# Fused linear attention and expert attention on one core: smaller q transfers, another q layout, g by a matmul, new orders

## The chip, the core and the metric

The kernel runs on one core of a Trainium2 chip. The core has a matrix engine (TensorE, PE in the profile), a vector engine (VectorE, DVE), a scalar engine (ScalarE, ACT), a general engine (GpSimd, POOL), an engine that only waits and issues transfers (SyncE, SP) and 16 DMA engines. Each engine works through its own list of instructions in order, and the engines meet at semaphores. The metric is the device time of one run in microseconds; lower is better.

## What is computed

Inputs are `q`, `k`, `v` of shape (8 batches, 8 heads, 576 tokens, 64), a norm weight `g_norm` of 64, and expert weights `w_gate` (512, 4), `wq`, `wk`, `wv` (4, 512, 64) and `wo` (4, 64, 512).

```
kv  = einsum('bhsd,bhse->bhde', k, v)
out = einsum('bhsd,bhde->bhse', q, kv)
x   = out / sqrt(mean(out*out, -1) + 1e-6) * g_norm        # heads joined: (8, 576, 512)
logits = x @ w_gate;  the two best of 4 experts per token, softmax over the two
for each expert e:
    a   = causal softmax((x @ wq[e]) @ (x @ wk[e]).T / 8)
    out += gate[e] * (a @ (x @ wv[e]) @ wo[e])
```

Each expert is an attention over all 576 tokens of a batch with one head of 64.

## The kernel before, in words

The work is cut into 1201 named tasks, each with a batch as its first number. Per batch: `lk`, `lv`, `lq` load; `kv` (two, `kv.b.n`) makes the 64x64 products on TensorE in fp32, `kvc` copies them out, `kgm` and `kgr` fold the gate weights in; `q` turns q on TensorE for batches 0 and 1 (`qc` copies the result), while for the other batches q comes in 32-float runs and `qc` turns it on VectorE; `out` multiplies by `kv`, five blocks of 128 tokens; `oc` copies, `sq` squares, `red` sums, `ln`, `rs` and three Newton steps `na`, `nb`, `nc` make the reciprocal root; `xm` scales, `x` turns on TensorE, `xc` copies. The gates are made from `gl`, `lg`, `m8` to `gate`. Then for two pairs of experts: `v`, `qp`, `kp` project, `sc` makes scores, `exp` and `msk` the masked exponentials, `pv` the weighted sums, `rc`, `iv`, `oc2` scale, `ot` turns, `y` multiplies by `wo`, `yc` copies, `st` stores.

Nothing is scheduled while the program is built. The string `ORDER` gives, two digits a task, the order in which the tasks are emitted, and so the order on every engine and on SP's queue of transfers. `ENGINE` gives for each task VectorE, ScalarE or GpSimd where it has a choice. `SLOTS` gives each buffer and each PSUM bank its place. A task waits for what it reads, and for the last user of the place that it writes. `ZEROS` names tasks before which TensorE gets a number of matmuls of zeros (128x512, bf16), written into the bank that the task writes next; they compute nothing that is used.

Loads are issued by SP (`lv` of batch 0 by ScalarE's queue). Batches 0 and 1 load k, v and q in two halves by head pair, in runs of 2304 bytes: nine tokens to a partition, so token 9p + j of a head lies in partition p at place j. All three `q_tr` of a batch read both halves. Batches 2 to 7 load k and v whole, and q in four quarters (32 partitions each, runs of 128 bytes). `gb` (L322) spreads the gate weights over the partitions with a matmul by a row of ones, and `wg` (L332) multiplies them by `g_wide`, which a transfer on GpSimd's queue fills in all 128 partitions (L197); `g8` (L318) scales `g_wide` and `g_rows` by 8. The weights `wq`, `wk`, `wv` are scaled by `g_rows` in `ws` (L345). Lines L267 and L270 are the helpers through which every matmul and every transpose of the end goes, L276 the one for copies, so in the profile the tiles tell them apart: `kvq` holds k, v, q and the turned q, `kvx` the products, `ident_f` is the fp32 identity that turns q.

Of the kernel before, what the change touches and what calls it, by code (L numbers as in the profile page):

```python
# [10 lines left out]
FP32 = mybir.dt.float32  # L11
# [12 lines left out]
    ('gb',): 19, ('q', 0, 2): 7, ('out', 0, 3): 9, ('q', 1, 2): 20, ('v', 0, 0): 1,  # L24
    ('sc', 0, 0, 0): 2, ('out', 1, 4): 6,
# [15 lines left out]
    "7J8pArAsANAd9HAt8t989I8uCQ9J99AO8vEJ8mAeASCRCE7MCIAh9ACFCMAfCJAgCUCGAiCNEKCKAjCVCH7PCOATELCS9KCLAU9L9MCPCWEO8w"
    "AoCT7SBMAp8y9N9PEM8x9O8zBNAw8+CXBK8-9QCYENAx9091CZAy9RBLCa92AkAzCb9S93AuAlCc9TGjBRCiB4AvGh9aBS9UCl9bCjB5EP9X9c"
    "BT9dCk9YCfCm9V9e9Z9gCrCnB79W9hB1B8BU9fGiB2CgB69iCsGgChD2B3CtBVCdD4D3D0D5D8D1BWCeBXA+D9B9BYBOCuA-BZEUCvCxEYCoCw"
    "BPGZCyEVB0EZEcBQCzEWC+GaC-EaEXEdEgEbGbEkEeEhCpElBAEiEfCqBbEmBCBBBDBfGcDCBEBgGeBhDcDDEjEnDaDdEoEpBFBaEqBGDbDAEr"
    "BcBHBdD6EsBeDBF2BIGfD7DnDhDoBJDHE-DiGdF3BiF4DIEtDkDEBjF0DlBtDjEuDJBnF1BuDpBqDmDFBoFMBvEyFKBrBpFNBkFLF8BsBwF5Bl"
    "EzBxBmDKE+F9DNDGByDeDLEvF6FIDODfFBGwF7DMFJGsGxFADPGkFCGtDgFDG+FEGlGuFFGoG-GvEwGmDrGpExDqGnDRGqFsDvDsGyGrDwDtGz"
    "H0FGDuFtFODxDQFHH1FPFqDSDVH2DTH3DWDUFSFrDXH4H5DYH6FTHCFQDZHFDyFRHDDzFxHEH9FuFyFUE7HID+FvE1D-E4FzE8E2HAFwE0E5H7"
    "HYE9HBHJHZE3FVHGHLE6HWHHEAHXHKFWFdFXEBFeHaH8FYECFfHcHOHMHRHbHPHdFZHQF+HNHSG1FaHTF-HUI8HVG2G0FbI6I9G3FcG5I7HgG9"
    "GAGBHiHhFgHjG4FhFiG6FjG7HeFkFlIDG8HfFmIEIGFnIAFoIBGCIFFpIJGDIKICIHHqHkILHnHrIIGHGNGIHoHsINGOGJGKHlHpIRGEGPGLIS"
    "IMGFITHmGQGMIOHtGRIPHwGGIQHuIWHvGSHyIXIUHzHxH+IVI2H-I0I3I1IbIYIcIeIZIdI4IfI5IaIkIhIgIlImIiIj"  # L50
)
ENGINE = (
    "VVVVVVVVVVVVVVVGVGVGVGVAVAVVVVVVVVVAVVVAVVAVVVGVVAAVVAAVVVGVAAVGVAAVGVAAVVVAAVVVAAVVVVVGVAGVAGVVGVVVVVVVAVVVVV"
    "VAVVVAVVVAVAVVVAGVAGVAGVAGVVVGVVGVVVVAVAVAGVAGVAGVAGVVVGVVGVVVVVVVAVVAVVVVVAVVVVVVVVVAGVGVVAVVVAVAAVVVAVVAGVVA"
    "AVVVAVAAVGVVVGVAGVAGVAGVVGVVVVAVVVVVVAVAVAVAVAVAVAVAGVAGVAGVAGVVVGVVVVVAVAVAVAGVAGVAGVAGVVVVVVVVVVVVVVAVVVVVVV"
    "VAVVVVVVVVVAGVVVVVVVVAGVVAAVVVAVVVGVVAAVAAVGVVVVVVGVVGVAVVAGVVVGAVGVVVVAVAVAVAVVVAVAVAGVAGVAGVAGVVVGVVGVVVVAVV"
    "VAGVAGVAGVAGVVVGVVGVVAVVVVAVVVVVAVVAVVVVVVVVVAGVGVVVVVVVGVVVGVVAAVVAGVVVGVAAVVVGVVVVGVAVVVGVAGVVVGAVGVVGVVVAVA"
    "VVVAVVVVVAGVAGVAGVAGVVVGVVGVVAVAVAVAGVAGVAGVAGVVVGVVVVVAVAVVAVVVVVVVVAVVVVVVVVVAGVGVVVVVVAGVVVAVVAAVVAAVVAGVAA"
    "VVVGVGVVVVAGVVGVVGVAVGAVGVVVVVVAVAVAVAVAVVVAGVAGVAGVAGVVVGVVVVVVVVVAVAGVAGVAGVAGVVVVVVGVVVVAVVVVVVVVVVVVVVVVVV"
    "VVVAGVGVVVVVVAAVVVAVVVAVVAGVVAAVAAVGVGVGVAGVVGVVVVAGVVVGAVVVVVVAVVVVVAVVVAVAVAGVAGVAGVAGVVVGVVGVVAVVVVVAGVAGVA"  # L60
    "GVAGVVVGVVGVVAVVVVVVVAVVAVVVVVVVVVVVVVVVGVVVVVVVAVVAAVVAGVVAGVVAAVAAVGVGVVVAGVVGVAGVVGVVVGAVGVVGVAVVVAVAVAVAVA"
    "VAGVAGVAGVAGVVVVVVVVVVVAVAVAGVAGVAGVAGVVVVVVVVVVVAVVVVVVVVVVVAVVVVVVVVVAVVGVVVVVVVGVVVAVVAAVVVAVVAAVAAVVVGVGVA"
    "VVVVVAGVAVVVVGAVGVVGVVVVVAVVVAVVVVVAGVAGVAGVAGVVVVVVGVVVVVVVVVVAGVAGVAGVAGVVVVVVGVVVVAVVVVAVVAVVVVVAV"
)
SLOTS = (
    "0120102341233450561677230120138021394A543B0102C30450106102101212011327603207301102102435202334015829BAC4163775"
    "40011132016752106123322013132081C4457671411037513200106200506131321300223145631440335102983BC415617110A7260127"
    "02231312520631020114312102161200432332649520376652B723010231021310320083321C0112011670072311047671B14AC5910305"
    "42136720132601132203103218012214025031545003452431071945BA2C302032301203012016170001166287060312726051742B1367"
    "1011297601230112231001106103223021067A2C61006111330010232248550174"  # L70
# [3 lines left out]
def loads(b):  # L74
    return range(EP) if b < 2 else range(1)


def names(nb):
# [3 lines left out]
    for b in range(nb):  # L82
        out += [(m, b, p) for p in loads(b) for m in ("lk", "lv")]
        out += [("lq", b, i) for i in (loads(b) if b in QPE else r4)]
        if b == 0:
            out += [("g8",), ("gb",), ("wg", 0), ("wg", 1)]
            out += [(m, nm, p) for nm in "qkv" for p in r2 for m in ("lw", "ws")]
            out += [(m, "o", p) for p in r2 for m in ("lwo", "wo")]
# [30 lines left out]
def kernel(  # L119
# [60 lines left out]
    def buf(key, shape, dtype, name):  # L180
# [7 lines left out]
    g_wide = const.tile([P, Dh], FP32, name="g_wide")  # L188
    ob = const.tile([P, NB, NCH, 2 * GW], FP32, name="o_sb")
# [4 lines left out]
    one_row = const.tile([1, Dh], FP32, name="one_row")  # L194
    nc.vector.memset(one_row[:], 1.0)
    nc.gpsimd.dma_start(wg_rows, moe_w_gate.rearrange("d e -> (d e)").unsqueeze(0))
    nc.gpsimd.dma_start(g_wide[:], g_norm.unsqueeze(0).to_broadcast([P, Dh]))  # L197
    nc.gpsimd.dma_start(
        g_rows[:], g_norm.rearrange("(p c) -> p c", c=NCH).unsqueeze(0).to_broadcast([P * NCH // Dh, Dh // NCH, NCH])
    )  # L200
# [107 lines left out]
    def lq(b, i):  # L308
        if b in QPE:
            load_nine(nc.sync, long("q", b), q, b, i)  # L310
            return
# [527 lines left out]
```

## Time and profile before

| what | value |
|---|---|
| median of 3 runs | 248.05 us (245.39 to 248.36) |
| the profiled execution's own time | 245.43 us |
| its span, first to last instruction | 243.6 us |
| mean granted TensorE clock | 0.934 |
| TensorE busy | 209.9 us, 86% |
| weight loads (overlap matmuls) | 170.8 us |
| VectorE, ScalarE, GpSimd busy | 163.1, 136.0, 112.5 us |
| matmuls of zeros | 64, 20.5 us |
| packets, bytes by DMA | 73225, 40.49 MB; 57024 packets under 512 B |
| read from and written to HBM | 30.45 MB, 9.44 MB |

Times in the profile are from one execution; its span starts at the first instruction. A row of a group gives the line in the kernel, the engine, what is written and read, how often, the busy time, the mean of one in ns, and the idle time ahead of it with what ended most of it. A busy share is an average over stages, so stages are read one by one. PE and PEld, matmuls and the loads of their stationary operand, are one list of instructions.

### The profile page before, as it was taken

To read this page: it belongs to the slowest core of one execution; us is meant where nothing else is said; L and a number is where in the kernel's file an instruction comes from. 1 tells how busy PE (TensorE), PEld (TensorE's weight loads), DVE (VectorE), ACT (ScalarE), POOL (GpSimd) and SP (SyncE) were. 2 spreads that over 40 slices of the span, in tenths; PEclk is the share of its full clock that TensorE was granted. 3 is DMA by queue.
4 is the path that set the end of the run, shared out by engine and by line. 5 is a ranking of instruction groups with operands and counts; after the bars stand their busy time and mean duration, and the time that the engine had idled before them with its cause. 6 is when DMAs were issued, how large, how long until landed. Compare 5 with 4: busy or idle time off the path is not lost.

```text
span 243.6 us, 9455 instructions
## 1 busy us (share of the span) xinstructions
PE 209.9 (86%) x4088; PEld 170.8 (70%) x4088; DVE 163.1 (67%) x408; ACT 136.0 (56%) x248; POOL 112.5 (46%) x203
## 2 busy tenths in 40 slices
PE   7948589799749779879998999699979999999992
PEld 2244438786616678879977968598869879889650
DVE  1066785315838934457999799379986889876582
ACT  2040615469615607733788378455875688793761
POOL 6007461018327237267456648243845673643330
PEclk9997979999968959689999999889999999999999
DMA  6999999999999969956981999600500050040055
GB/s 228 203 379 180 312 231 250 224 263 183 336 174 210 238 120 259 262 68 203 142 186 41 341 159 253 199 4 0 194 6 5 1 196 4 3 183 13 1 196 194
DMA packets 73225, 40.49 MB, mean 166 GB/s; under 512 B 57024, under 2 KB 59600, under 8 KB 73184
## 3 DMA queue, kind: packets, MB, share of 16 engines
q1 hardware_dynamic: 72544, 38.67, 63.9%
q10 hardware_dynamic: 544, 1.18, 1.3%
q0 software_dynamic: 96, 0.04, 1.2%
q8 instruction: 32, 0.52, 1.0%
q14 instruction: 9, 0.07, 0.1%
HBM read 30.45 MB, written 9.44 MB: 164 GB/s over the span
## 4 chain that ended last, share of the span: by engine, by line
PE 76%; issue 10%; DMA 5%; DVE 4%; ACT 3%; SPq 0%; ACTq 0%
PE p L267 74%; DMA kvq<-in_q_dram 5%; ACT PT L624 2%; PE p L270 2%; DVE osc L672 1%; DVE tmp L276 1%; DVE kvq L276 1%; DVE xT L276 1%; DVE OT L276 0%; DVE ms L446 0%; ACT qTp L276 0%; ACT o_sb L276 0%; ACT sq L440 0%; SPq L295 0%; DVE inv L661 0%
## 5 line engine op out<-in xcount | busy, mean ns | idle before, releaser
L624 ACT ACTIVATE PT<-p 128x1024 bf16<-128x1024 f32 (+1 forms) x64 | 50.3, 845 | 4.4 <-PE p L267 3.5
L630 POOL TENSOR_SCALAR_AFFINE_SELECT PT<-PT 128x256 bf16<-128x256 bf16 (+1 forms) x80 | 30.0, 395 | 36.5 <-ACT PT L624 36.3
L498 POOL TENSOR_TENSOR tmp<-o_sb,rstd 128x512 fp32r<-128x512 f32 x29 | 33.0, 1193 | 15.2 <-DVE rstd L477 9.7
L267 PE MATMUL p<-kvq,kvq 64*64 64x64 f32 x1152 | 23.3, 234 | 9.1 <-issue 9.0
L267 PE MATMUL p<-wv_r,xT 128*128 128x256 f32 x160 | 26.3, 300 | 2.4 <-issue 1.7
L267 PEld LDWEIGHTS p<-kvq,kvq 64*64 64x64 f32 x1152 | 21.2, 147 | 10.2 <-issue 9.8
L446 DVE TENSOR_REDUCE ms<-sq 128x8 f32<-128x520 f32 (+1 forms) x40 | 26.3, 678 | 1.9 <-POOL sq L442 1.4
L267 PE MATMUL p<-kvx,kvq 64*64 64x68 f32 x1152 | 24.3, 228 | 3.1 <-issue 3.1
L267 PEld LDWEIGHTS p<-kvx,kvq 64*64 64x64 f32 x1152 | 22.2, 139 | 5.3 <-issue 3.8
L267 PE MATMUL p<-ident_r,tmp 128*128 128x128 f32 (+1 forms) x160 | 24.6, 287 | 0.7 <-ACT PT L624 0.7
L267 PE MATMUL p<-zeros 128*128 128x512 bf16 x64 | 20.5, 480 | 5.4 <-issue 3.6
L442 POOL TENSOR_TENSOR sq<-o_sb 128x512 f32<-128x512 f32 (+1 forms) x15 | 15.5, 1038 | 20.5 <-ACT o_sb L276 10.2
L267 PEld LDWEIGHTS p<-ident_r,tmp 128*128 128x128 f32 x160 | 21.4, 198 | 4.3 <-issue 2.7
L267 PEld LDWEIGHTS p<-wv_r,xT 128*128 128x128 f32 x160 | 21.8, 196 | 3.5 <-issue 2.0
L276 ACT COPY o_sb<-p 128x544 f32<-128x544 f32 (+1 forms) x23 | 13.5, 609 | 18.0 <-PE p L267 17.6
L267 PE MATMUL p<-qTp,kT 64*128 64x64 f32 (+4 forms) x192 | 22.0, 344 | 0.7 <-ACT PT L624 0.7
L267 PE MATMUL p<-wo_b,OT 128*128 128x512 bf16 (+1 forms) x96 | 21.1, 375 | 1.5 <-DVE OT L276 0.9
L267 PE MATMUL p<-xT,wk_r 128*128 128x288 f32 x128 | 20.9, 312 | 0.0
L267 PE MATMUL p<-xT,wq_r 128*128 128x288 f32 x128 | 19.7, 299 | 0.0
L276 DVE COPY o_sb<-p 128x544 f32<-128x544 f32 (+1 forms) x17 | 12.0, 715 | 10.6 <-PE p L267 10.3
L267 PEld LDWEIGHTS <-zeros 128*128 128x128 bf16 x64 | 7.1, 119 | 16.9 <-issue 11.6
L267 PEld LDWEIGHTS p<-xT,wk_r 128*128 128x128 f32 x128 | 18.8, 201 | 0.3
(87 smaller groups left out, 354.9 us busy)
## 6 DMA issues: line engine op xcount, KB each, us to landing
out_dram<-tmp SPq DMA_DIRECT2D x32, 256.0 KB, 2.5
kvq<-in_q_dram SPq DMA_DIRECT2D x24, 288.0 KB, 8.0
kvq<-in_k_dram SPq DMA_DIRECT2D x6, 1152.0 KB, 8.1
kvq<-in_v_dram SPq DMA_DIRECT2D x6, 1152.0 KB, 7.3
kvq<-in_q_dram SPq DMA_DIRECT2D x4, 576.0 KB, 9.8
kvq<-in_k_dram SPq DMA_DIRECT2D x4, 576.0 KB, 11.1
kvq<-in_v_dram ACTq DMA_DIRECT2D x2, 576.0 KB, 9.2
kvq<-in_v_dram SPq DMA_DIRECT2D x2, 576.0 KB, 9.4
```

The source lines that it names most:

```text
L267: done.append(nc.tensor.matmul(*args, **kwargs))
L270: done.append(nc.tensor.transpose(*args))
L276: rd_(nc.scalar.copy(dst, src) if engine[task] == "A" else nc.vector.tensor_copy(out=dst, in_=src))
L442: nc.gpsimd.tensor_tensor(out=dst, in0=src, in1=src, op=AluOpType.mult)
L446: nc.vector.tensor_reduce(mss[b % 2][:nt, i, :], sqs[(NB * b + i) % 3][:nt], axis=AX_X, op=AluOpType.add)
L498: ew(("xm", b, i)).tensor_tensor(out=short("x", b, i, dtype=FP32R)[:].rearrange("p (c m k r) -> p m k r c", c=NCH, m=NCH, k=2), in0=ob[:, ...
L624: rd_(nc.scalar.activation(PT[:, :, d0 : d0 + o], big("sc", b, pr, j)[:, :, 0:o], ACTF.Exp, scale=scale))
L630: nc.gpsimd.affine_select(out=d, in_=d, compare_op=AluOpType.is_ge, fill=0.0, base=0, pattern=[[0, 2], [1, w]], channel_multiplier=-1,)
L672: rd_(nc.vector.tensor_tensor(out=osc[:, qc : qc + n, :, :].rearrange("p n e f -> p (n e) f"), in0=po[:, :, 0:Hd], in1=iv.rearrange("p n e ...
```

## The change

Five things change.

- `g_norm` comes into one partition (`g_row`). A new task `gg` spreads it with a matmul by ones into PSUM, and `g8` scales it from there into `g_wide`; a new task `g9` scales `g_rows`.
- q of batches 2 to 7 is loaded in eight transfers of 144 KB (two heads of a group each) where there were four of 288 KB; the runs stay 128 bytes.
- q of batches 0 and 1 is loaded in three parts of 192 tokens, each with two transfers (one for every half of the partitions) in runs of 768 bytes: three tokens to a partition. Token 192j + 3p + e lies in partition p. `q_tr` for part i reads that part alone, and writes PSUM with a step of three floats (`e::3`), so that the tokens stand in order there and `q_copy` reads and writes runs in order.
- `ORDER`, `ENGINE` and `SLOTS` are new throughout. TensorE's list now begins `gb` (14 zeros), `gg`, `kv.0.1`, `q.0.1`, `q.0.0` (6 zeros), `kv.0.0` (2), `q.0.2`, `out.0.2` (5), three more `out.0`, `q.1.2`, `out.0.4`, `x.0.0` (12), `q.1.0` (2), `x.0.2`, `v.0.0`, `kv.1.1`, the other `x.0`, `v.0`, `kp.0`, `qp.0`, two `sc`, `kv.1.0`, `q.1.1`. Before it began `gb` (19), the three `q.0` (7), both `kv.0`, `out.0` (9), the three `q.1` (20), two `x.0`, `kv.1.0`. SP's list begins `lk.0.1`, `lq.0.1`, `lq.0.0`, `lk.0.0`, `lq.0.2`, `lw.v.1`, `lw.k.1`, `lw.q.0`, `lq.1.2`, `lw.v.0`, `lw.q.1`, `lq.2.5`, `lk.1.1`, `lw.k.0`, `lq.1.0`, `lv.1.1`, `lk.1.0`, three eighths of `lq.2`, `lq.1.1`, `lq.3.7`, `lv.1.0`; nine transfers and weights later comes `lk.2.0`. On VectorE `qc.1.2` stands between `red.0.0` and `red.0.1`.
- 48 matmuls of zeros in nine places replace 64 in seven; `ot` may have them too.

```diff
 ZEROS = {
-    ('gb',): 19, ('q', 0, 2): 7, ('out', 0, 3): 9, ('q', 1, 2): 20, ('v', 0, 0): 1,
-    ('sc', 0, 0, 0): 2, ('out', 1, 4): 6,
+    ('gb',): 14, ('q', 0, 0): 6, ('kv', 0, 0): 2, ('out', 0, 2): 5, ('x', 0, 0): 12,
+    ('q', 1, 0): 2, ('sc', 0, 1, 2): 2, ('ot', 0, 1): 3, ('y', 0, 3): 2,
 }
...
-        out += [("lq", b, i) for i in (loads(b) if b in QPE else r4)]
+        out += [("lq", b, i) for i in (range(3) if b in QPE else range(8))]
         if b == 0:
-            out += [("g8",), ("gb",), ("wg", 0), ("wg", 1)]
+            out += [("gg",), ("g8",), ("g9",), ("gb",), ("wg", 0), ("wg", 1)]
...
+    g_row = const.tile([1, Dh], FP32, name="g_row")
...
-    one_row = const.tile([1, Dh], FP32, name="one_row")
+    one_row = const.tile([1, P], FP32, name="one_row")
     nc.vector.memset(one_row[:], 1.0)
+    nc.gpsimd.dma_start(g_row[:], g_norm.unsqueeze(0))
     nc.gpsimd.dma_start(wg_rows, moe_w_gate.rearrange("d e -> (d e)").unsqueeze(0))
-    nc.gpsimd.dma_start(g_wide[:], g_norm.unsqueeze(0).to_broadcast([P, Dh]))
...
     def lq(b, i):
         if b in QPE:
-            load_nine(nc.sync, long("q", b), q, b, i)
+            dst = long("q", b)[:].rearrange("p (m j x) -> p m j x", m=NCH, j=3)
+            src = q[b].rearrange("(m a) (j p e) d -> a j p m (e d)", a=2, j=3, p=NP)
+            for a in range(2):
+                nc.sync.dma_start(dst[a * Dh : (a + 1) * Dh, :, i, :], src[a, i])
             return
-        h0, a = NCH * (i // 2), i % 2
+        r, c0, n = i % 4, i // 4 * 2, 2 * (S // 32)
+        h0, a = NCH * (r // 2) + c0, r % 2
         nc.sync.dma_start(
-            long("q", b)[i * 32 : (i + 1) * 32].rearrange("p (x d) -> p x d", d=32),
-            q[b, h0 : h0 + NCH, :, a * 32 : (a + 1) * 32].rearrange("h (g t) d -> t (h g) d", t=32),
-        )
+            long("q", b)[r * 32 : (r + 1) * 32, c0 * S : (c0 + 2) * S].rearrange("p (x d) -> p x d", d=32),
+            q[b, h0 : h0 + 2, :, a * 32 : (a + 1) * 32].rearrange("h (g t) d -> t (h g) d", t=32),
+        )
+
+    def gg():
+        mm(small("gg")[:, 0:Dh], lhsT=one_row[0:1, :], rhs=g_row[0:1, :], start=True, stop=True)

     def g8():
-        for t in (g_rows, g_wide):
-            nc.vector.tensor_scalar_mul(out=t[:], in0=t[:], scalar1=float(Dh**0.5))
+        rd_(nc.vector.tensor_scalar_mul(out=g_wide[:], in0=small("gg")[:, 0:Dh], scalar1=float(Dh**0.5)))
+
+    def g9():
+        nc.vector.tensor_scalar_mul(out=g_rows[:], in0=g_rows[:], scalar1=float(Dh**0.5))
...
     def q_turned(b, i):
-        return big("qt", b, i)[:, :, 0 : 6 * NP].rearrange("p a (n j t) -> p a n j t", n=EP, j=3)
+        return big("qt", b, i)[:, :, 0 : 6 * NP].rearrange("p a (n t) -> p a n t", n=EP)

     def q_tr(b, i):
         t, p_t = nine(tiles["L", "q", b]), q_turned(b, i)
         for n in range(EP):
-            for j in range(3):
+            for e in range(3):
                 for a, o, rows, cols in quarters():
                     mm(
-                        p_t[cols, a, n, j, :], lhsT=t[rows, n + EP * o, 3 * i + j, :], rhs=ident_f[rows, rows],
+                        p_t[cols, a, n, e::3], lhsT=t[rows, n + EP * o, 3 * i + e, :], rhs=ident_f[rows, rows],
                         start=True, stop=True, skip_group_check=True,
                     )
...
-        dst = t[:].rearrange("p (n a t j) -> p a n j t", n=EP, a=2, j=NJ)[:, :, :, 3 * i : 3 * i + 3, :]
+        dst = t[:].rearrange("p (n a j t) -> p a n j t", n=EP, a=2, j=3)[:, :, :, i, :]
...
-        if n[0] in ("x", "v", "y"):
+        if n[0] in ("x", "v", "y", "ot"):
             t = small(*n)
```

## The prediction

> **What bounds the kernel now.** I read the page's busy shares and slices first, then a table of stages, the waits, the chain and the transfers.
>
> ```profile
> PE 209.9 (86%) x4088; PEld 170.8 (70%) x4088; DVE 163.1 (67%) x408; ACT 136.0 (56%) x248; POOL 112.5 (46%) x203
> ...
> PEclk9997979999968959689999999889999999999999
> DMA  6999999999999969956981999600500050040055
> ```
>
> TensorE leads. DMA is full for about 110 us, and the clock is low in that same stretch. The table has each stage's length, busy time by engine, granted clock, DMA share and GB/s:
>
> ```profile
> 0.00:13.68 13.68, 10.52 (x34) 3.61 (x35) 1.96 (x16) 1.28 (x1) 3.90 (x17) 1.00 0.86 237
> 13.68:39.09 25.41, 19.15 (x605) 12.90 (x605) 17.14 (x34) 8.97 (x18) 11.46 (x13) 0.87 1.00 259
> 75.00:110.00 35.00, 29.07 (x626) 27.02 (x627) 21.03 (x50) 18.46 (x36) 16.79 (x24) 0.80 0.90 196
> 160.00:227.30 67.30, 65.60 (x1090) 57.70 (x1083) 55.92 (x144) 46.13 (x84) 34.57 (x67) 1.00 0.16 55
> ```
>
> From 160 us TensorE has work at full clock all the time, so whatever it loses earlier moves the end. Its waits:
>
> ```profile
> PE p L267 <- issue: 17.5, 8, 3.6
> PE p L270 <- issue: 4.1, 1, 4.1
> PE p L267 <- ACT PT L624: 2.3, 5, 0.7
> PE p L267 <- DMA kvq<-in_q_dram: 1.9, 1, 1.9
> ```
>
> "issue" is a wait for no semaphore, and it is nearly all of the idle time. These stops come in the middle of groups (after one of five transposes of `ot`, for example). The trace gives them a rule: counted in weight loads, matmuls and waits, all the long ones stand at records 449, 961, 1473, 2497, 3009, 3777, 4801, 5569 and 6593, which is 193 plus a multiple of 256. They sum to 23.5 us from start to start. Each ends 1.3 to 1.7 us after a packet of the instruction queue:
>
> ```profile
> q8 instruction: 32, 0.52, 1.0%
> ```
>
> That is 16 KB a packet, 32 packets for 8228 records: 256 records each. A packet starts mostly 2 to 4 us after the boundary before it has been crossed while DMA is full (mostly 0 to 2 us later on). A block made of 64x64 matmuls alone runs in 2.1 to 2.9 us and so outruns it. What such a stop does is seen in the timeline:
>
> ```profile
> 31.58 5.32 PE L267 MATMUL p<-zeros 128*128 128x512 bf16 x18 [3.58 <-issue]
> 36.84 2.33 PE L267 MATMUL p<-ident_f,kvq 64*64 64x64 f32 x144
> 39.09 1.11 PE L267 MATMUL p<-ident_r,tmp 128*128 128x64 f32 x8
> ```
>
> The zeros before `q.1.2` run after the stop they were meant to fill. Batch 1's q had landed at 27.64 and the first `xm` was done at 33.0, yet batch 0's `x` starts at 39.1.
>
> **What the skill says.** "Runtime: NRT & Kernel Launch", Instruction fetch mechanics: refills of 16 KiB, 256 instructions, through a DMA queue. The trace agrees (193 + 256k); it does not agree that this is "mostly hidden". "TensorE: Matmul & The Clock Gate", Part 1: an idle window of about 3.4 us halves the clock. The trace has half clock for 3.4 or 6.8 us after the stops at 28, 66 and 84 us. "PSUM — Partial Sum Buffer", Specifications: lines of 8 bytes, and a non-contiguous pattern "slows matmuls significantly"; no row of before shows one.
>
> **Part by part.** *g.* The broadcast of `g_wide` goes. Its 16 packets took 1.51 us on average, and between 7 and 8 us only 4 load packets started where 138 to 174 did in each of the 4 us before. Worth 1.5 us for every later load. `gg` adds four records to TensorE and puts `g8` behind `gb`; it is ready at about 9.6 us, before `g9`'s data (12.59), so it costs nothing.
>
> *Loads.* Packets took 108 ns (2304 B), 57 ns (1024 B), 18 ns (128 B): a half of k or v is 256/16 x 108 = 1.7 us, a w 0.9, an eighth of q 1.3 (before: a quarter 2.6, so the sum is unchanged). For 768 B I estimate 46 ns between these rows (43 to 57): 4.4 us for a batch against 3.5. Batch 0, whole at 17.42 before with one w (0.9) ahead, is whole at 17.4 - 0.9 - 1.5 + 0.9 = 16. From there in SP's order `lv.1.1` lands at about 29, `lv.1.0` at 39, `lk.2.0` at 54. SP issues 60 q transfers for 28, 0.5 us each, hidden while DMA is behind; what then counts is that each load waits for the landing of the one eight places ahead (so the built program).
>
> *Start.* The first work needs only half of k and v, which take the places that landed at 6.25 and 6.73. 14 zeros at 0.43 us, `gb` 1.9, `gg`: `kv.0.1` runs at 9.6 (before: q at 13.68). Now the blocks decide. Boundary 193 lies at the end of `kv.0.1`, 10.7 us. With before's delays of crossing to crossing where a refill binds (4.8 to 6.5 us), 449 (in `kv.0.0`) is passed at 15.5, 705 (in `out.0.2`) at 20.8, 961 (in `q.1.2`) at 26.2. `out.0` is done by 27 against 27.4. So the earlier data is largely lost to refills.
>
> *`x` of batch 0.* VectorE has `qc.1.2` between its reductions, so `red.0.1` and all behind it (the Newton steps, `xm`) wait for `q.1.2`, 26.7 us. Then `qc` 1.0, two `red` 0.68 each, three small steps: `nc.0.0` at 29.5; `xm.0.0` 1.2: 30.7. TensorE has 12 zeros there, 2.6 us warm to 4.3 half cold after 27.0, so `x.0.0` starts at 31 (before 39.1). VectorE then needs two `red`, eight small steps, `xm.0.2`, two `ws` (0.74), `xm.0.1` (1.2), `vc`, `qc.1.0`, `xc.0.1`, `xm.0.4`: until about 40. `x.0.4` 40.5, its copy 41.1, four projections of 1.15 and one v: 46.4, two `sc`: 47. Before had this, and `q.1.1` besides (0.8), at 52.5. **Gain 4.7 us.** Of `kv.1` each has one half behind it.
>
> *Strided PSUM writes.* Six `q_tr` at 0.78 us. At most double by the two-float line: 4.7 us; batch 0's three lie in waits for data, so 0 to 2.3 on the path. I take 0.5. In return the copies write in order: 1.55 us for 768 elements now, about 0.9 to 1.0 by the 544-element row (0.61 on ACT, 0.72 on VectorE); counted above.
>
> *Zeros.* After this point before has 8 more (2.1 us), after 7 shorter waits of which some are filled: 0.6 gained. Those before `q.1.2` went into the 4.7. Zeros cannot fill a fetch stop, so "all longer gaps" is not what they reach.
>
> *Later stops.* Dense blocks (over 220 of 256 records of `kv`, `out`, `q`): before had stops of 4.36, 3.31, 1.78 and then 0, 0.97, 2.60, 1.92, 0, in all 14.9. After has blocks ending at 1729, 2497, 3009, 4033 in the full stretch (2.6, 1, 3.3, 2.5, from block time against 5.5) and about 2 at 1985 and 2241, and six later at before's mean of 1.1: 18.0. **Cost 3.1.** What it may give back is the clock: `y.0` took 4.5 us at half clock (0.7 of it a wait) against 2.3 for `y.1`, and 75 to 110 us ran at 0.80 (7 us lost). Smaller stops around 62 to 70 us leave `y.0` and `x.1` warm: I take 4.2 of these (0 to 9).
>
> Sum: 4.7 - 0.5 + 0.6 - 3.1 + 4.2 = 5.9. The profiled run's own time is 245.43 (span 243.6, 1.8 around it), so 239.5; the median of the three runs is 1.0107 times the profiled one, so **242.0**.
>
> **Rivals.** *More returns* (0.22): the clock stays up and DMA, rid of `g_wide`, refills sooner: another 5 to 8 us, 235. The stops stand for it, the number of dense blocks against. *Fetch takes it all* (0.13): the twelve dense blocks stop 4 us each while DMA is full; 247. The change then does not do what its zeros and orders are for. *The transfer queue runs dry* (0.17), the slower side: SP is in order, and blocked for a buffer (it stood 9.5, 8.8 and 11.6 us at 27, 46 and 63) it has eight eighths ahead, 10 us of work, where it had eight quarters, 21. TensorE reaches `kv.2.1` at about 62 with `lk.2.0` at 54, slack 8. If the DMA share of the first 60 us falls below 0.87, TensorE waits; at 0.71 it waits 9.4 and runs 3.4 us at half clock: 242 + 9.4 + 1.7 = 253. Full shares up to 108 us speak against. The forecast itself has 0.48, of which 0.31 below 243.1.
>
> **Numbers.** 2% (about what this kernel's measurement can tell from no change) is 243.1 and 253.0. Faster 0.31 + 0.22 = 0.53, same 0.17 + 0.13 = 0.30, slower 0.17. Range 233 (more returns at its best) to 252, leaving out most of the dry queue.
>
> **What would show it.** First `kv` matmuls at 9 to 10 us; no 2048-byte packets on the software queue; all long stops at 193 + 256k; `x.0` from 31, projections done by 47; DMA share near 1.0 to 100 us; `q_tr` still near 0.78 us. It fails if stops fall elsewhere, if `x.0` waits for VectorE well past 31, or if `kv` waits for k or v.

## The result, and the profile after

| | before | after |
|---|---|---|
| median of the runs, us | 246.77 (245.39 to 248.36, 4 runs) | 258.28 (256.24 to 258.89, 4 runs) |
| ratio, 95% interval | | 1.045 (1.035 to 1.055) |
| span of the profiled execution, us | 243.6 | 257.2 |
| mean granted TensorE clock | 0.934 | 0.933 |
| stops of TensorE that no semaphore explains, summed | 19.9 us, 8 stops | 33.3 us, 13 stops |

The change makes the kernel 4.5% slower; 242.0 was forecast, with a range up to 252. Ratios and intervals leave out slow runs, those over 1.5% above the quickest of the same kernel, unless they are said to be "by resampling", which takes all runs. The last row counts every gap over 0.25 us between the end of one matmul or weight load and the start of the next where the trace shows no semaphore.

The page of the changed kernel: busy times, the slices of clock and transfers, two queues, and the chain that ended last by engine.

```profile
PE 207.5 (81%) x4060; PEld 173.8 (68%) x4074; DVE 158.0 (61%) x399; ACT 138.9 (54%) x257; POOL 110.0 (43%) x203
...
PEclk9889777998999999989999599986999999999999
DMA  6999999999827999941949927993130041040046
...
q8 instruction: 32, 0.52, 1.0%
q0 software_dynamic: 96, 0.01, 0.3%
...
PE 63%; issue 16%; DVE 7%; DMA 6%; ACT 4%; POOL 2%; SPq 1%; DVEq 0%; POOLq 0%; ACTq 0%
```

TensorE works 2.4 us less than before and is still the longest engine; its share fell from 86% to 81% because it stands still more. The broadcast is gone from the software queue (0.3% for 1.2%), and there are as many instruction packets as before. Full stretches of transfers now last to about 175 us, where before the last load lands at 153.5, and they break off in places, longest from 109 to 122 us. TensorE's waits (us in total, times, longest):

```profile
PE p L270 <- issue: 34.1, 18, 5.8
PE p L270 <- DMA o_sb<-in_moe_w_gate_dram: 2.4, 1, 2.4
```

Where the time goes is read from four stages, cut where TensorE ends the projections of batches 0, 1 and 4. Columns: the stretch, its length, busy time of PE, PEld, DVE, ACT, POOL, granted clock, DMA share, GB/s. The kernel before:

```profile
0.00:51.80 51.80, 40.29 (x784) 26.79 (x784) 25.04 (x68) 16.20 (x29) 16.62 (x31) 0.93 1.00 260
51.80:95.10 43.30, 34.68 (x834) 28.10 (x833) 26.45 (x61) 23.22 (x44) 21.14 (x31) 0.84 0.97 213
95.10:167.80 72.70, 66.69 (x1380) 59.44 (x1379) 54.73 (x134) 44.92 (x84) 38.59 (x68) 0.93 0.74 162
167.80:243.60 75.80, 68.20 (x1099) 56.46 (x1096) 56.88 (x147) 51.61 (x91) 36.12 (x74) 0.99 0.23 80
```

The changed kernel:

```profile
0.00:55.00 55.00, 38.17 (x719) 28.06 (x723) 22.53 (x66) 13.42 (x31) 14.91 (x31) 0.88 1.06 217
55.00:93.80 38.80, 31.96 (x876) 27.44 (x879) 27.61 (x56) 23.90 (x45) 18.25 (x27) 0.96 0.82 202
93.80:182.40 88.60, 69.88 (x1386) 61.88 (x1386) 53.83 (x135) 49.37 (x90) 38.90 (x70) 0.90 0.74 165
182.40:257.20 74.80, 67.50 (x1086) 56.42 (x1089) 53.98 (x143) 52.19 (x93) 37.94 (x75) 1.00 0.23 81
```

So +3.2, -4.5, +15.9 and -1.0 us. In the third stage TensorE stands idle 18.7 us for 6.0 before, and 16.7 us of that are five such stops, for 4.7 in three before; the other 3.2 us are busy time, at a clock of 0.90 for 0.93. The worst stop is in the `kv` and `out` matmuls of batches 5 and 4. The timeline of TensorE there (start, length, operation, count, and the idle time before it):

```profile
129.93 2.21 PE L270 MATMUL p<-kvq,kvq 64*64 64x64 f32 x134
133.78 0.39 PE L270 MATMUL p<-kvq,kvq 64*64 64x64 f32 x10 [1.65 <-issue]
133.95 1.98 PE L270 MATMUL p<-kvx,kvq 64*64 64x68 f32 x118
141.72 1.41 PE L270 MATMUL p<-kvx,kvq 64*64 64x68 f32 x26 [5.79 <-issue]
```

Between the two stops lie 256 records, ten matmuls of `kv` and 118 of `out` with a weight load each. They run in 2.2 us, and then nothing is there to run for 5.8 us. The refill packet had started 5.0 us after the boundary at 133.8. (A boundary is the start of a block of 256 records; a refill is the packet of the instruction queue that brings the block after it; the rings, further down, are the lists of transfers that wait for the DMA engines.)

### The profile page after: what moved, and what is told of

It is laid out like the page before. It is cut to its first block, busy times and chain, and to the rows that moved or that the text cites. A ratio compares the mean times of both kernels' runs of the same rounds, so it can differ in the third digit from the quotient of the medians.

```text
span 257.2 us, 9446 instructions
## 1 busy us (share of the span) xinstructions
PE 207.5 (81%) x4060; PEld 173.8 (68%) x4074; DVE 158.0 (61%) x399; ACT 138.9 (54%) x257; POOL 110.0 (43%) x203
## 4 chain that ended last, share of the span: by engine, by line
PE 63%; issue 16%; DVE 7%; DMA 6%; ACT 4%; POOL 2%; SPq 1%; DVEq 0%; POOLq 0%; ACTq 0%
PE p L270 61%; DMA kvq<-in_k_dram 5%; ACT PT L636 2%; POOL tmp L510 2%; PE p L273 1%; DVE osc L684 1%; SPq L316 1%; DMA out_dram<-tmp 1%; DVE ms L458 1%; ACT tmp L279 1%; DVE rstd L489 1%; ACT xT L279 1%; DVE inv L673 1%; DVE tmp L510 1%; POOL tmp L396 0%
## 5 line engine op out<-in xcount | busy, mean ns | idle before, releaser
L270 PE MATMUL p<-kvx,kvq 64*64 64x68 f32 x1152 | 27.4, 243 | 13.5 <-issue 12.9
L270 PEld LDWEIGHTS p<-kvx,kvq 64*64 64x64 f32 x1152 | 24.9, 152 | 15.4 <-issue 13.5
L279 ACT COPY o_sb<-p 128x544 f32<-128x544 f32 (+1 forms) x28 | 16.6, 611 | 27.6 <-PE p L270 27.2
L270 PEld LDWEIGHTS p<-kvq,kvq 64*64 64x64 f32 x1152 | 20.0, 139 | 16.8 <-issue 16.1
L454 POOL TENSOR_TENSOR sq<-o_sb 128x512 f32<-128x512 f32 (+1 forms) x19 | 19.7, 1038 | 15.3 <-ACT o_sb L279 9.1
L270 PEld LDWEIGHTS p<-ident_r,tmp 128*128 128x128 f32 x160 | 20.8, 190 | 4.8 <-POOL tmp L510 3.0
L270 PE MATMUL p<-xT,wk_r 128*128 128x288 f32 x128 | 22.5, 323 | 1.0 <-DVE ms L458 0.7
L396 POOL TENSOR_TENSOR tmp<-kvx,wg_t 128x512 f32<-128x512 f32 x8 | 11.1, 1398 | 22.8 <-DVE kvx L279 17.9
L270 PEld LDWEIGHTS p<-xT,wk_r 128*128 128x128 f32 x128 | 19.6, 208 | 1.8 <-DVE ms L458 0.8
L673 DVE RECIPROCAL inv<-p 128x6 f32<-128x6 f32 (+1 forms) x32 | 5.9, 185 | 22.6 <-PE p L270 22.1
L270 PE MATMUL p<-vext,PT 128*128 128x65 bf16 x480 | 19.3, 201 | 0.2
L270 PEld LDWEIGHTS p<-qTp,kT 64*128 64x128 f32 x192 | 14.5, 185 | 7.1 <-DVE kvx L403 1.4
```

Source lines behind the costliest of these rows:

```text
L270: done.append(nc.tensor.matmul(*args, **kwargs))
L279: rd_(nc.scalar.copy(dst, src) if engine[task] == "A" else nc.vector.tensor_copy(out=dst, in_=src))
L396: ew(("kgm", b, m)).tensor_tensor(out=short("g", b, m)[:].rearrange("p (e f) -> p e f", e=E), in0=kvx[b % 2][:, m, E : E + 2 * Dh].unsquee ...
L454: nc.gpsimd.tensor_tensor(out=dst, in0=src, in1=src, op=AluOpType.mult)
L673: rd_(nc.vector.reciprocal(iv.rearrange("p n e -> p (n e)").unsqueeze(2), po[:, :, Hd : Hd + 1]))
```

## Experiments

The kernel before ran beside each group of experiments on the same chip, and the medians are given beside each other. In some groups its runs lay wide apart (238.0 to 251.7 us over 35 runs), so the intervals there are worked out by drawing anew from all runs of both kernels and taking the ratio of medians; this is said as "by resampling". Each experiment has one profiled execution, and single stops differ between executions, so one stop alone proves little.

### The order or the parts

`parts_only`: the order, slots and zeros of before, all three parts put in.

```diff
-            load_nine(nc.sync, long("q", b), q, b, i)
+            for j in {(0, 1): (2, 0), (0, 0): (1,), (1, 0): (2, 0), (1, 1): (1,)}[b, i]:
+                for a in range(2):
+                    nc.sync.dma_start(dst[a * Dh : (a + 1) * Dh, :, j, :], src[a, j])
...
+        for c0 in (0, 2):        # each quarter of q as two eighths, one after the other
...
+    gg, g8, g9 as in the change, gg after gb
```

> The order and the zero matmuls of the kernel before, with all three parts of the change: g by a matmul (w_gate fetched second), q of batches 2 to 7 in eighths, q of batches 0 and 1 in thirds of 768-byte runs with strided PSUM writes. Theory 'order' (the new order of the work lengthens the instruction-fetch stops): 241 to 248 us, no slower than before, fetch stops near the 21.6 us of before. Rival 'parts' (the smaller transfers, the 768-byte runs, the strided writes or the g matmul cost the time): 254 to 260 us, as the changed kernel.

`order_only`: the kernel before with `ORDER`, `ENGINE`, `SLOTS` and `ZEROS` of the change.

```diff
-ORDER, ENGINE, SLOTS, ZEROS of before
+those of the change, without gg, g9 and the second eighth of each quarter;
+lq.0.1, lq.0.0, lq.1.2, lq.1.0 load the halves, lq.0.2 and lq.1.1 nothing
```

> The changed kernel's order, engines, slots and zero matmuls, with none of the three parts: g broadcast by DMA, q of batches 2 to 7 in quarters (each issued where the first of its two eighths stood), q of batches 0 and 1 in two halves of 2304-byte runs, PSUM written in order. Theory 'order': 254 to 262 us, with fetch stops of about 33 us in all. Rival 'parts': 245 to 249 us, with stops near 22 us.

Beside 244.92 us of before, `parts_only` took 249.22 (ratio 1.022, 1.012 to 1.033; 1.018 by the medians) and `order_only` 252.18 (1.032, 1.024 to 1.041). Neither theory had it: by the medians they cost 4.3 and 7.3 us, and the sum is near the 11.5 of the change. The cost of the parts is the less certain of the two, as the runs further down show. In `order_only` TensorE has only 16.7 us of fetch stops, and in return waits 8.0 us for q. Its loss lies in the third stage all the same: 82.3 us for 72.7.

### Is it the instruction fetch, and where its boundaries lie

`shift128`:

```diff
-        for _ in range(count):
-            mm(t[:, :], lhsT=zeros[:, 0:P], rhs=zeros[:, 0:512], ...)
+        w = 512 if n != ("gb",) else 92        # and ZEROS: ('gb',): 14 -> 78
+        for _ in range(count):
+            mm(t[:, 0:w], lhsT=zeros[:, 0:P], rhs=zeros[:, 0:w], ...)
```

> The changed kernel with its 14 zero matmuls of 512 columns ahead of the first work replaced by 78 of 92 columns: the same length of time, 128 more instruction records, so that every 256-record boundary falls half a block earlier in the work. Theory 'fetch': all stops over 1.5 us without a semaphore again stand at records 193 + 256k, so they move to other tasks (the 5.8 us stop at the end of the batch-4 out group and the 4.9 us stop in out of batch 6 are gone from there), and the time changes by several us, 250 to 264. Rival 'program waits' (the stops belong to those tasks or to their buffers): they stay at the same tasks, with the same 5.8 and 4.9 us, and the time stays within 1 us of 258.

258.83 us (1.059, 1.051 to 1.066). All 14 stops stand at records 193 + 256k, now in other tasks. TensorE's timeline at the place of the 5.8 us stop:

```profile
136.44 1.77 PE L269 MATMUL p<-kvx,kvq 64*64 64x68 f32 x90 [1.02 <-issue]
138.14 1.30 PE L269 MATMUL p<-vext,PT 128*128 128x65 bf16 x37
142.78 0.43 PE L269 MATMUL p<-vext,PT 128*128 128x65 bf16 x5 [3.35 <-issue]
```

The 5.8 us stop is gone from its place in `out`, where 1.0 us stands some matmuls earlier, and 3.4 us sit in `pv`. The time alone would have fitted the rival too; the places decide. So these are fetch stops, and not waits of a task. In all kernels run here every stop above 0.5 us stands at such a record (or, where a trace lacks a few matmul records, that many earlier).

`before_shift120` makes the same move in the kernel before:

```diff
-        for _ in range(count):
+        for w in [64] * (68 if n == ("gb",) else 0) + [512] * count:   # ('gb',): 19 -> 11
```

> The kernel before with the first 19 zero matmuls of 512 columns replaced by 68 of 64 columns and 11 of 512, in a stretch where TensorE waits for data: 120 records more, the work, its order and its transfers unchanged. A sum over the records of the kernel before, with a refill ready 5.7 us after the boundary before it where the transfer rings are full, 4.4 where half full and 3.6 where quiet, gives 23 us of stops unshifted and 33 us with a shift of 120. Theory 'boundaries': 251 to 258 us, stops above 28 us. Rival 'order' (what makes stops is the order of the work, wherever the boundaries lie): 244 to 248 us.

256.10 us beside 246.28 (1.040, 1.033 to 1.057 by resampling). TensorE's waits:

```profile
PE p L266 <- issue: 23.9, 13, 3.8
PE p L266 <- DVE ms L445: 2.4, 1, 2.4
...
PE p L266 <- DVE tmp L497: 1.8, 1, 1.8
```

120 records ahead of any work cost almost as much as the whole change, without one instruction moved. The time was forecast well, its composition less so: stops rose by 4 us, not 10. The rest comes as waits for VectorE (2.4 and 1.8 us above) and as 4.7 us more busy time, in part at a lower clock. `after_shift184` tries it the other way on the changed kernel:

```diff
+        for w in [64] * (103 if n == ("gb",) else 0) + [512] * count:   # ('gb',): 14 -> 3
```

> The changed kernel with 103 zero matmuls of 64 columns and 3 of 512 in place of its first 14 of 512: 184 records more. The same sum over its records gives 29 us of stops unshifted and 26 to 23 near this shift. Theory 'boundaries': 3 to 6 us faster than the changed kernel, 251 to 256 us. Rival: no gain, 257 to 260 us.

257.01 us (255.06 to 260.57), as the rival had it: nothing certain was gained. The trace is mixed: the four stops up to 33 us sum to 5.7 us instead of 10.8, and the projections of batch 0 end at 49.6 instead of 55.0. But stops of 5.7, 2.7 and 3.2 us then come between 134 and 174 us. A better place for the boundaries at one end is a worse one at the other.

`parts_aligned` asks whether `parts_only` loses only by its 6 extra records:

```diff
-    ('gb',): 19,
+    ('gb',): 16,        # in parts_only
```

> The kernel before with all three parts of the change, as in the run parts_only (249.2 us, ratio 1.022), and with 16 instead of 19 zero matmuls ahead of the first work: 6 instruction records fewer, which the g matmul had added, so that every 256-record boundary lies in the same task as in the kernel before. Theory 'boundaries' (what the parts cost is mostly that they shift the boundaries by 6 records): 241 to 246 us, with the 4.9 us stop in kv.0.0 back near 2.7. Rival 'parts' (they cost it by their own transfers and writes): 248 to 251 us.

248.57 us beside 246.28 (1.009, 1.003 to 1.024 by resampling), and the stop in `kv.0.0` is still 4.3 us. The theory of the boundaries was wrong for the parts; the time is where the rival had it.

### Do transfers lengthen the stops

`light_after`:

```diff
-            q[b, h0 : h0 + 2, :, a * 32 : (a + 1) * 32].rearrange("h (g t) d -> t (h g) d", t=32),
+            q[b, h0 : h0 + 2].rearrange("h s d -> (h s d)").rearrange("(a p x d) -> a p x d", a=2, p=32, d=32)[a],
```

> The changed kernel with q of batches 2 to 7 fetched as contiguous runs of 4608 bytes instead of 128-byte packets (the same bytes into the same places, so q's layout, and with it the result, is not that of the reference). Theory 'fetch under DMA load': the refill packets that started 4.2 to 6.1 us after their boundary start within about 2.5 us, the stops at 142 and 174 us fall from 5.8 and 4.9 to under 2.5 us, all stops together to below 22 us, and the time to 236 to 247 us. Rival 'fetch regardless of DMA' (a refill takes as long with quiet engines): stops of the same lengths, 33 us in all, time 252 to 258 us.

256.36 us (1.044, 1.034 to 1.054); stops 29.0 us in all, of which 5.2 at record 4801. The theory's 236 to 247 was missed, and the time lies in the rival's range. Small packets are not the cause. But the rings were as full where it mattered: the late refill for 4801 (4.6 us) met a DMA share of 0.88 made of long packets.

`no_late_loads` takes transfers away instead; it leaves out every load of batches 6 and 7:

```diff
     def lk(b, p):
+        if b > 5:
+            return
...
-        kt, vt = nine(tiles["L", "k", b]), nine(tiles["L", "v", b])
+        kt, vt = nine(tiles["L", "k", five(b)]), nine(tiles["L", "v", five(b)])   # five(b) = min(b, 5); lv, lq, qc alike
```

> The changed kernel without the loads of batches 6 and 7: their work is done on the tiles of batch 5 (so their output is not the reference's), the order and the number of TensorE's records are the same, and the transfer rings are quiet from about 130 us. Theory 'fetch under DMA load' (a refill waits for the transfers that stand in the rings): the refills at 134 and 167 us start about 1 us after their boundary instead of 5.0 and 4.2, the stops fall from 5.8 and 4.9 us to 1 to 2 each, and the time falls by 7 to 10 us, to 248 to 252. Rival 'fetch regardless of DMA': these two stops stay above 4 us, time 255 to 258.

251.10 us beside 246.28, 7.2 us below the changed kernel, as the theory had it. TensorE's timeline for the same instructions as above:

```profile
134.19 2.21 PE L269 MATMUL p<-kvq,kvq 64*64 64x64 f32 x134
137.75 0.39 PE L269 MATMUL p<-kvq,kvq 64*64 64x64 f32 x10 [1.36 <-issue]
137.92 1.98 PE L269 MATMUL p<-kvx,kvq 64*64 64x68 f32 x118
142.40 0.82 PE L269 MATMUL p<-kvx,kvq 64*64 64x68 f32 x26 [2.49 <-issue]
```

5.79 us became 2.49, the 4.9 us stop became 1.36, and the matmuls after the stop ran at full speed (0.82 us for 1.41). Over the 14 traces in which no matmul record is missing, counting the refills that start after TensorE reaches the boundary, the picture is this: with a DMA share above 0.8 in the 2 us after a boundary the refill packet starts some 2.8 us after it on average (over 220 refills, up to 7.0); below 0.5 it starts after 1.0 us (some 150 refills, none above 2.3). TensorE goes on 1.5 us after the packet's end (1.2 to 1.8 over some 155 stops).

A full share is not the whole of it. After the boundary at 137.75 us in `no_late_loads` the DMA share was still 1.3, nearly all of it packets of 128 bytes, and the refill started after 1.7 us instead of 5.0; only the boundary at 163.9 us met quiet rings (share 0.04, 0.9 us). Sorted by what fills the rings, the refills with a share above 0.8 start after 1.7 us on average where packets of 768 to 4608 bytes have less than a tenth of the transfer time (40 refills, single ones up to 7.0), and after 3.3 us where they have over nine tenths (116). `light_after`, in which nearly all packets are long, has 3.7 us over its 16 refills with full rings, where the other 13 traces have 2.4 to 3.1. So late refills go with long packets (k, v and the first q here) more than with short ones; with one execution a run this is likely and not proven.

Why are there loads at 134 and 167 us at all? The timeline of SyncE's queue in the changed kernel (start, time to issue, count):

```profile
104.37 5.58 SPq L320 DMA_DIRECT2D kvq<-in_q_dram  x3
120.25 2.06 SPq L727 DMA_DIRECT2D out_dram<-tmp  x4
...
143.62 0.50 SPq L320 DMA_DIRECT2D kvq<-in_q_dram  x1
154.29 3.49 SPq L727 DMA_DIRECT2D out_dram<-tmp  x6
157.84 2.42 SPq L320 DMA_DIRECT2D kvq<-in_q_dram  x3
```

It stands before the stores of batch 1 from 110.0 to 120.3 us, and before those of batch 2 from 144.1 to 154.3, each time with loads behind. At the stores of batch 1 the kernel before stands 3.4 us:

```profile
111.54 9.55 SPq L313 DMA_DIRECT2D kvq<-in_q_dram  x4
124.44 2.42 SPq L715 DMA_DIRECT2D out_dram<-tmp  x4
```

Two runs take this up. `after_quarters` joins the eighths again:

```diff
+        if (b, i) in [the second eighth of each quarter]:
+            return
-        h0, a = NCH * (r // 2) + c0, r % 2
+        h0, a = NCH * (r // 2), r % 2          # the whole quarter, where its first eighth stood
```

> The changed kernel with q of batches 2 to 7 in quarters, each issued where the first of its two eighths stood; records and boundaries unchanged. Theory 'late loads' (the eighths put the second half of each quarter behind the stores of batch 1, so transfers meet the refills at 134 and 167 us): the stops of 5.8 and 4.9 us fall to about 2 and 1.5, the time to 251 to 254. Rival 'start' (what the parts add lies in the first 55 us): 256 to 259.

253.48 us (252.65 to 257.02) beside 246.88 of before (1.027, 1.018 to 1.054 by resampling), 4.8 below the changed kernel; but two of the five runs took 257, as the changed kernel does, so the size of the gain is uncertain. The same four lines of TensorE's timeline:

```profile
130.00 2.20 PE L269 MATMUL p<-kvq,kvq 64*64 64x64 f32 x134
133.97 0.39 PE L269 MATMUL p<-kvq,kvq 64*64 64x64 f32 x10 [1.76 <-issue]
134.14 1.98 PE L269 MATMUL p<-kvx,kvq 64*64 64x68 f32 x118
138.62 0.82 PE L269 MATMUL p<-kvx,kvq 64*64 64x68 f32 x26 [2.50 <-issue]
```

At `kv` of batch 5 both profiled executions are at the same place (129.9 and 130.0 us); behind it lies the gain of the profiled one (252.65 us). The last load lands at 165.3 instead of 176.4, and the refill at 163 us starts after 1.1 us instead of 4.2. The run does not separate the size of the transfers from the earlier place of their second halves. `loads_first` moves loads alone:

```diff
 ORDER: ahead of st.1.1
+lq.4.3 lq.5.7 lq.5.0 lq.5.3 lq.5.4 lq.5.1 lk.6.0 lq.6.1 lq.6.3 lq.6.0 lq.6.2 lq.6.7 lq.6.4 lq.7.5
```

> The changed kernel with 14 loads (q of batches 4 to 6, one of batch 7, k of batch 6) moved ahead of the stores of batch 1 in SyncE's list, nothing else. Theory 'late loads behind stores': SyncE no longer stands still with loads behind it from 106 to 120 us, the loads are all landed some 8 to 10 us sooner, the refill at 167 us (4.2 us late) finds quiet rings, and the time falls by 3 to 6 us, to 252 to 255. Rival (the stores are not what makes them late, or the loads then meet other refills): 256 to 260.

260.88 us (256.57 to 263.96): no gain, as the rival had it, and just above the rival's range. The transfers no longer pause at 113 us, and the two stops shrank to 3.6 and 2.2 us. But loads still stood behind the stores of batch 2 and went out from 156 us, and the stop at 167 us grew from 0.8 to 3.2. The profiled execution has the span of the changed kernel, 257.2 us. So the two large stops come and go with the loads there, but freeing loads from the stores of batch 1 did not pay: that the place behind the stores costs the time is argued, not shown.

### The start

`after_halves` gives batches 0 and 1 their halves back, `after_g` the broadcast:

```diff
-            for a in range(2):
-                nc.sync.dma_start(dst[a * Dh : (a + 1) * Dh, :, i, :], src[a, i])
+            half = {(0, 1): 1, (0, 0): 0, (1, 2): 1, (1, 0): 0}.get((b, i))
+            if half is not None:
+                load_nine(nc.sync, long("q", b), q, b, half)        # and q_tr, q_copy of before
```

> The changed kernel with q of batches 0 and 1 in two halves of 2304-byte runs and PSUM written in order; boundaries within 1 record. Rival 'start': TensorE waits some 8 us for q, but its three early fetch stops (10.8 us together) mostly vanish in that wait, batch 0's projections are done 3 to 5 us sooner, time 253 to 256. Theory 'late loads': 256 to 260, the later stops unchanged.

```diff
-    nc.gpsimd.dma_start(g_row[:], g_norm.unsqueeze(0))
     nc.gpsimd.dma_start(wg_rows, moe_w_gate.rearrange("d e -> (d e)").unsqueeze(0))
+    nc.gpsimd.dma_start(g_wide[:], g_norm.unsqueeze(0).to_broadcast([P, Dh]))        # no gg; ('gb',): 14 -> 17
```

> The changed kernel with g broadcast by DMA again and w_gate fetched first, 17 instead of 14 zero matmuls ahead of the first work, so the boundaries lie in the same tasks within 2 records. The forecast's step (the broadcast costs every load 1.5 us) gives 258 to 261; the rival (w_gate first lets the first work begin 2 us sooner, and fetch takes what the loads gain) 255 to 258.

255.09 us (252.38 to 258.89) and 255.64 (251.01 to 257.71), beside 246.88. Both fell where their rivals had them, and both end batch 0's projections sooner, at 52.2 and 50.7 us instead of 55.0. Both keep the late stops (4.7 and 5.2, 4.4 and 5.2 us). Each range touches that of the changed kernel, so 2 to 3 us is a possible gain, not a certain one. Nor does the sooner end speak for these two parts: in `after_quarters` and `light_after`, which leave batches 0 and 1 as in the change, batch 0's projections end at 50.5 and 52.9 us, in `no_late_loads` at 57.1.

### Each part alone, and two together

`g_only`, `eighths_only` and `runs768_only` are the three pieces of `parts_only`, each alone in the kernel before; `two_parts` has the eighths and the 768-byte runs, without g.

```diff
+gg, g8, g9 as in the change; ('gb',): 19 -> 16        # g_only
+for c0 in (0, 2): ...                                 # eighths_only, two_parts
+thirds, p_t[cols, a, n, e::3], the copies             # runs768_only, two_parts
```

> The kernel before with the g matmul alone (w_gate fetched second), and 16 instead of 19 zero matmuls ahead of the first work, so that the 256-record boundaries lie in the same tasks within 2 records. All three parts together cost 2 to 4 us. The forecast's step (the broadcast's packets are gone, 1.5 us for every load) gives 243 to 245 us, 1 to 2 us below before; the rival (w_gate lands later and the first loads do not come sooner) 246 to 249.

> The kernel before with q of batches 2 to 7 in eighths alone. The forecast's step (the same packets, so no cost) gives the time of before within 1 us; the rival (a queue that holds eight transfers holds half the bytes, loads come later and meet other refills) 2 to 4 us more, 247 to 250.

> The kernel before with q of batches 0 and 1 in 768-byte runs and strided PSUM writes alone, boundaries within 2 records of before. The forecast's step (0.5 us for the writes, 0.9 us more transfer for each batch, less for the copies) gives 0 to +1.5 us; the rival (the start is what the parts cost: q later, and a longer fetch stop in kv.0.0) +2 to +4 us, 247 to 250.

> The kernel before with the eighths and the 768-byte runs (strided PSUM writes too), without the g matmul; boundaries within 2 records of before. Alone they stood at 244.5 and 244.3 us beside 246.1. If the parts add up: 242 to 244 us, faster than before by 1 to 1.5%. If they only move the transfers against the refills: anything from 244 to 250, most likely within 1% of before, with stops that differ from those of either alone.

Beside 246.13 us of before (35 runs): g 245.98 (0.999, 0.991 to 1.005 by resampling), eighths 244.51 (0.993, 0.986 to 1.000), 768-byte runs 244.28 (0.992, 0.981 to 1.015). Without resampling the ratios on record are 1.011 (1.001 to 1.022), 1.020 (1.014 to 1.025) and 0.986 (0.976 to 0.996). The two ways of counting do not agree even on the sign for the first two, so within some 2% no part alone shows a cost or a gain. The g matmul does what was said of it: the last half of k for batch 0 lands at 16.16 us instead of 17.42. No gain in time is seen from it.

`two_parts` took 243.45 us beside 248.25: ratio 0.983 (0.973 to 0.993), and 0.981 (0.974 to 1.007) by resampling. It is the best version here, but that it beats the kernel before is likely and not shown. TensorE's waits in it:

```profile
PE p L266 <- issue: 17.5, 10, 2.7
PE p L266 <- ACT PT L628: 2.5, 6, 0.7
```

Its longest fetch stop is 2.7 us, and none over 1 us begins between 33 and 98 us, where before has 4.1 and 3.1. With the g matmul added these two parts stand at 1.009 (`parts_aligned`), with stops of 3.9, 3.4 and 3.1 us there. Why a part that shows no cost alone should cost that beside the others was not settled; it was only seen that the stops of every variant fall differently.

### The zero matmuls

`narrow_zeros` and `two_parts_narrow` leave every zero matmul in place and cut it to 2 columns:

```diff
-            mm(t[:, :], lhsT=zeros[:, 0:P], rhs=zeros[:, 0:512], ...)
+            mm(t[:, 0:2], lhsT=zeros[:, 0:P], rhs=zeros[:, 0:2], ...)
```

> The changed kernel with each of its 48 zero matmuls cut from 512 to 2 columns: the same records and boundaries, hardly any filling. If the zeros keep the clock up and cover the gaps, as they are meant to, the time rises by 3 us or more, to above 261. If what they cover is set by the fetch in any case, it stays within 2 us of 258.

> The run two_parts (0.983 of before) with each of its 64 zero matmuls cut from 512 to 2 columns, records and boundaries unchanged. If zeros keep the clock up where the wait is one for data (up to 13.7 us, and before q.1.2): 246 to 250, slower than two_parts by 1% or more. If they bring nothing anywhere: 0.975 to 0.99 of before, as two_parts or a little below it.

In the changed kernel nothing is lost: 255.93 us (254.86 to 259.07) for 258.28, close to the second expectation. TensorE's timeline of the changed kernel shows why; the 12 zeros ahead of `x.0.0` come after the stop:

```profile
30.80 0.77 PE L270 MATMUL p<-ident_f,kvq 64*64 64x64 f32 x23
36.51 0.92 PE L270 MATMUL p<-ident_f,kvq 64*64 64x64 f32 x25 [4.94 <-issue]
37.21 1.12 PE L270 MATMUL p<-kvx,kvq 64*64 64x68 f32 x16
38.67 3.98 PE L270 MATMUL p<-zeros 128*128 128x512 bf16 x11 [0.33 <-DVE kvq L279]
42.30 0.74 PE L270 MATMUL p<-ident_r,tmp 128*128 128x128 f32 x4
```

And `narrow_zeros`:

```profile
37.86 0.48 PE L269 MATMUL p<-zeros 128*128 128x2 bf16 x12
40.61 1.12 PE L269 MATMUL p<-ident_r,tmp 128*128 128x128 f32 x4 [2.27 <-POOL tmp L509]
```

The zeros held `x.0.0` back: `xm.0.0` had ended at 41.0, the zeros ran on to 42.3. The granted clock from 20 to 45 us was 0.50 without them for 0.80, and that cost nothing on balance. In the order of before they seem to matter: `two_parts_narrow` took 248.34 us beside 246.64 (1.011, 1.004 to 1.019; 1.007, 0.999 to 1.016 by resampling), where `two_parts` stands at 0.983. The 19 zeros ahead of `gb` stand in a real wait for data there (with narrow ones TensorE waits 5.8 us for `w_gate`). What they bring is open: up to 45 us the clock is no lower with narrow zeros (1.00 for 0.88 up to 20 us, 0.89 for 0.83 from there).

## Why the prediction was wrong

**The bound held.** TensorE bounds the kernel, and its large gaps are stops of the instruction fetch at 193 + 256k. `shift128` shows the rule and `no_late_loads` the dependence on transfers. The forecast's own warning, that zeros cannot fill such a stop, was right too. What failed is the sizing of the stops, in two steps; together they miss by 13.7 us (4.7 of gain against a loss of 3.2, and a cost of 3.1 against 8.9), of the 19.5 between the forecast's gain of 5.9 and the loss of 13.6 in the profiled spans.

**The start: "with before's delays of crossing to crossing where a refill binds (4.8 to 6.5 us)".** This is the first step that failed. The crossings were forecast for 10.7, 15.5, 20.8 and 26.2 us and came at 12.0, 19.6, 27.9 and 36.5: 7.5, 8.3 and 8.7 us each. The refill packets started 4.7, 4.8 and 6.1 us after the boundary; at the same records of the kernel before it was 2.4, 2.3 and 4.1. The forecast had taken the range of a few stops in one execution for a law, and the other runs spread these delays up to 7.0 us. Why these three came so late stays open: long packets filled the rings there, but at record 193 they did so in the kernel before too.

**`x` of batch 0.** The chain was right, link by link: VectorE waits for `q.1.2`, and reductions, Newton steps and `xm` wait behind it. VectorE's timeline:

```profile
37.50 0.96 DVE L279 COPY kvq<-p 128x768 f32<-128x768 f32 x1 [5.99 <-PE p L270]
```

It sits idle for 6.0 us and gets `q.1.2` at 37.4 instead of 26.7. So `x.0.0` starts at 42.3, not 31, and the gain of 4.7 us became a loss of 3.2. The size of this loss holds for the profiled execution: in the other runs with this order the projections of batch 0 end between 49.6 and 57.1 us (before: 51.8), but in none by the 47 of the forecast.

**Later stops, "18.0. Cost 3.1".** Second failure. After 40 us they sum to 22.5 us, for 13.6 in the kernel before: the term cost 8.9 us and not 3.1. The blocks up to record 4033 took 9.0 us for the 11.4 in the forecast; the six later ones, priced "at before's mean of 1.1", took 13.6 for 6.6. Two of these, at records 4801 and 5825, took 5.8 and 4.9 us. The mean came from an execution whose last load lands at 153.5 us; in the changed kernel it lands at 176.4. The forecast had no term for this: it priced the eighths by their bytes, and followed SyncE's queue only to `lk.2.0`. `after_quarters` puts 4.8 us on the eighths in this order, of uncertain size, and `no_late_loads` 7.2 on all the loads of the last two batches; in the order of before the eighths show no clear cost of their own. How much of it comes from the waits of SyncE before stores stays open, since `loads_first` brought no gain.

**The give-back of the clock, 4.2 us.** It came in part: from 55 to 94 us the clock was 0.96 for 0.84, and TensorE's busy time there fell by 2.7 us; the rest of the stage's 4.5 us is less idle time. The next stage gave it back, with 3.2 us more busy time at 0.90 for 0.93. Over the span the clock is 0.933 for 0.934, so over both stages this term came to about nothing.

**Small terms.** *g*: in `g_only` k landed 1.3 us sooner where 1.5 was said, with no gain in time to be seen. "It costs nothing" missed that `w_gate` is now fetched second: `gb` waited 2.4 us and `kv.0.1` began at 10.5, not 9.6. *768-byte packets*: 61 ns on average, not 46 (range 43 to 57), so batch 0 was whole at 19.0 us, not 16. *Strided PSUM writes*: a `q_tr` took 0.93 us at full clock for 0.78, so 0.9 us for all six, well inside the bounds; "PSUM — Partial Sum Buffer", Specifications, calls such a pattern a significant slowdown, and the measured 19% decides here. *Copies*: 0.9 to 1.0 us was said:

```profile
L279 DVE COPY kvq<-p x4: 942/954/958, 16.4 to 58.3; 128x768 f32<-128x768 f32 x4
```

*Zeros*: 0.6 us was booked as a gain; `narrow_zeros` shows none.

**The rivals.** "Fetch takes it all" named the mechanism and stopped at 247, since it let the late blocks off. "The transfer queue runs dry" was the slower case and is not what happened: DMA was full for the first 55 us and `kv.2.1` did not wait for its loads. SyncE's list did fall behind, but what followed was loads beside late stretches of dense matmuls and not a TensorE without data.

## What to carry to other kernels

Where a kernel has stretches of tiny matmuls, count records: a block of 256 that runs in 2.3 us cannot outlast a refill of about 3.5 us with quiet rings (1.0 us to the packet, 1.0 for the packet, 1.5 until TensorE goes on) or 5.6 us with full ones (2.8, 1.3 and 1.5), so spread such stretches between long matmuls and check where big transfers fall against them. Price a change in transfer sizes also by where each piece then stands in its queue and what runs when it lands, and not by its bytes alone. In such a kernel compare a change with neutral shifts of the same program (some dozens of tiny matmuls ahead of the work) before crediting or blaming it: here one shift of 120 records was worth 4%.

## What the runs showed of the hardware

- Refills come later beside other transfers: 1.0 us from boundary to packet below a DMA share of 0.5, 2.8 above 0.8, up to 7.0; with full rings 1.7 beside short packets and 3.3 beside packets of 768 bytes and more. The skill's page "Runtime: NRT & Kernel Launch", Instruction fetch mechanics, has the fetch mostly hidden; here 16 to 33 us of each execution are fetch stops.
- 120 records of idle matmuls at the start made an unchanged kernel 4% slower.
- Half clock for 25 us (0.50 from 20 to 45 us in `narrow_zeros`) cost nothing on balance where fetch stops of 3.3, 1.2 and 4.3 us fell in and around the same stretch.
